# Attention backward on one core: the token stage takes heads four apart, in longer DMA pieces, and ScalarE copies the memory columns

## Chip, cores, metric

The kernel runs on one core of one Trainium2 chip. The metric is the device time of one execution in microseconds, the median of several runs. Engines are named as in the profile: PE (TensorE matmul), PEld (its weight loads), DVE (VectorE), ACT (ScalarE), POOL (GpSimd), SP (SyncE). A "q" behind a name is that engine's instruction queue, which also issues DMAs.

## What is computed

The reference is a gated mix of two attentions over 2048 tokens of width 576, and the gradients of everything but one input. The part that the change touches is the second, a recurrent one with memory:

```python
# H = 32 heads of 128, M = 8 memory rows, segments of 32 tokens (64 segments)
for s in range(n_seg):
    h = concatenate([mem, xs], axis=1)              # 8 memory rows and 32 tokens
    q, k, v = h @ Wq, h @ Wk, h @ Wv                # per head
    p = softmax(where(mask, q @ k.T * scale, -1e9)) # tokens causal, memory seen by all
    o = (p @ v) @ Wo
    mem = o[:, :M]
    outs.append(o[:, M:])
```

The first, A, is plain softmax attention with 32 query heads of 18 and one key and value head. The output is `g * a + (1 - g) * b`, and the kernel returns it with eleven gradients.

## The kernel before

The work is a row of stages, each a hand-ordered program (`manual_schedule`): projections; the memory recurrence forward woven with A's first pass; the **token stage** `b_bulk` (L662); the recurrence backward `b_chain_bwd` (L998) woven with A's second pass `a_pass2` (L1893); then the rest of the gradients. Matrices that do not fit into the chip's memory lie in DRAM tensors between the stages.

The token stage does attention B for the 32 tokens of each segment, forward and backward. Its unit is a *step*: one token tile of 128 tokens (four segments) and four heads. There are 16 tiles x 8 head groups = 128 steps, and `order` (L914) gives, for turn t, which parts of which steps run: a part with lag n works on step t - n, so up to six steps are in flight. A part transposes q, k, dO, v on PE (`trans`, L768), makes scores S against the tokens (diagonal 32x32 blocks) and against the memory columns (`score`, L782), takes exp on ACT (`st_S`), masks and sums on DVE, makes the probabilities P on POOL (`st_R`, L807), the output o and the gradient dq (`attend`, L762), dS on POOL (`st_Y`, L874), and the gradients of the memory rows of k and v (`st_K`, `st_KE`, L893, L901). For every tensor index 0 of P and dS is the tokens' half and index 1 the memory's.

Four steps are a *chunk*: 16 heads of one token tile. Inputs come by chunk, in 512 KB DMAs with 4 KB per token row (`load`, L676): q, dO, k into rings of four, v into three buffers. Memory rows come as `mB` (L693), four DMAs each for k and v, one per place i of a head in its step, into the block of 32 partitions that i owns; memory columns as `mT` (L690), one DMA for each tile and tensor. Results leave by chunk: o, dq (4 KB a row), px and dsx (the tokens' half of P and dS), and the memory gradients dm (four DMAs, L907). Which load follows which part stands in `after` (L917); stores are put on a list (`due`) and issued on SP at the end of the next turn by `flush` (L728), on ACT in the last turns. SP issues in program order.

`mem_T` (L744) transposes on PE the memory's half of P of one step and of dS of another into free columns of the score bank, and copies both to x_mT; `attend_m` (L757) uses x_mT as weights, with mB as the moving side. A step's heads are neighbours: step g of a tile takes heads 4g to 4g + 3, so a chunk's P tile has the order (step, half, place, key).

At the end, `a_pass2` starts with the load of b_KV (L1901) and the first b_QS (L1911), and `b_chain_bwd` reads the memory gradients in `load_c` (L1031).

Of the kernel before, what the change touches and what calls it, by code (L numbers as in the profile page):

```python
# [16 lines left out]
P = 128  # L17
# [29 lines left out]
class Kern:  # L47
# [290 lines left out]
    def b_chain_fwd(self, keep, sp, psum):  # L338
# [69 lines left out]
        for s in range(NSEG):  # L408
# [21 lines left out]
            def mT_store(w):  # L430
                nc.gpsimd.dma_start(self.mTd[w][s], mT[w][:].rearrange("p c u t -> p (c u) t"))
# [230 lines left out]
    def b_bulk(self, wp, vp, kp, sp, psum):  # L662
# [51 lines left out]
        def view(t):  # L714
            return t // 8, t % 8, slice(4 * (t % 4), 4 * (t % 4) + 4), C[t // 4]
# [3 lines left out]
        def store(t, dst, src):  # L719
            if t % 4 == 3:  # L720
                tt, h0 = t // 8, 16 * (t // 4 % 2)
                if len(dst.shape) == 4:
                    due[1].append((dst[tt][:, h0:h0 + 16, :].rearrange("p (a i) k -> p a (i k)", i=4),
                                   src[:, :, 0].rearrange("p a i k -> p a (i k)")))
# [14 lines left out]
        def transp(x, nm):  # L739
            o = sp.tile([P, 4, 32], BF16, name=nm, bufs=2)  # L740
            nc.vector.transpose(o[:].rearrange("p i k -> p (i k)"), x.rearrange("p i k -> p (i k)"))
            return o

        def mem_T(t):  # L744
# [6 lines left out]
            for j, n, w in u:  # L751
                self.tr(pt[:, j, :], C[n // 4][w][:, n % 4, 1].rearrange("p i k -> p (i k)"), P)
                sc[w + "mT", n] = mt[:, j, :]
            js = slice(u[0][0], u[-1][0] + 1)
            nc.vector.tensor_copy(mt[:, js, :], pt[:, js, :])

        def attend_m(t, w, m):  # L757
            po = sc["po" + w, t] = psum.tile([P, 4, P], F32, name="x_po", bufs=2)
            self.mm(po[:].rearrange("p i e -> p (i e)"), lhsT=sc.pop((w + "mT", t)), rhs=m.rearrange("p i e -> p (i e)"),
                    start=True, stop=False)  # L760
# [7 lines left out]
        def trans(t, w, nb):  # L768
            tt, g, r, d = view(t)
# [12 lines left out]
        def score(t, ps, l4, r4, w, part):  # L782
            tt, g, r, d = view(t)
            for i in range(4):
                if part:
                    self.mm(ps[:, 1, i, :], lhsT=l4[:, i, :], rhs=mT[tt][w][:, :, 4 * g + i, :])
# [14 lines left out]

        def st_M(t):
# [4 lines left out]
        def st_R(t):  # L807
            tt, g, r, d = view(t)
# [5 lines left out]
            o = chunk(t, "P", [P, 4, 2, 4, 32], 3)  # L814
            nc.gpsimd.tensor_tensor(out=o[:, t % 4], in0=Et[:], in1=bc(rl[:]), op=ALU.mult)
            store(t, self.px_dram, o)

        def st_T(t):
            sc["PT", t] = transp(view(t)[3]["P"][:, t % 4, 0], "x_PT")

        st_Om = lambda t: attend_m(t, "P", mB["v"][t // 4 % 2][:, t % 4])
        st_Qm = lambda t: attend_m(t, "dS", mB["k"][t // 4 % 2][:, t % 4])

        def st_O(t):
            tt, g, r, d = view(t)
            o = chunk(t, "o", [P, 16, P], 2)
            attend(o[:, r, :], t, "P", sc.pop(("PT", t)), d["v"][:, r, :])
            store(t, self.xtok["o"], o)

        def st_OT(t):  # L830
            tt, g, r, d = view(t)
            pt = psum.tile([P, 4, P], BF16, name="x_tr", bufs=2)
            for i in range(4):
                self.tr(pt[:, i, :], d["o"][:, 4 * (g % 4) + i, :], P)
# [5 lines left out]
        def st_B(t, a):  # L840
            tt, g, r, d = view(t)
# [3 lines left out]
            for i in (2 * a, 2 * a + 1):  # L845
                for hf in range(2):
                    self.mm(pb[tt][:, hf, 0:288], lhsT=oT[:, i, :], rhs=self.WoN[:, 4 * g + i, 288 * hf:288 * hf + 288],
# [16 lines left out]
        def st_D(t):  # L864
            tt, g, r, d = view(t)
# [3 lines left out]
            nc.vector.scalar_tensor_tensor(out=flat(X[:]), in0=flat(ps), scalar=SCALEB, in1=flat(d["P"][:, t % 4]),  # L869
# [4 lines left out]
        def st_Y(t):  # L874
            tt, g, r, d = view(t)
            Y = sp.tile([P, 2, 4, 32], F32, name="x_Y", bufs=1)
            nc.gpsimd.tensor_tensor(out=Y[:], in0=d["P"][:, t % 4], in1=bc(sc.pop(("dl", t))[:]), op=ALU.mult)
            o = chunk(t, "dS", [P, 4, 2, 4, 32], 3)
            nc.gpsimd.tensor_tensor(out=o[:, t % 4], in0=sc.pop(("X", t))[:], in1=Y[:], op=ALU.subtract)
            store(t, self.dsx_dram, o)  # L880

        def st_DT(t):
            sc["DT", t] = transp(view(t)[3]["dS"][:, t % 4, 0], "x_DT")

        def st_Q(t):
            tt, g, r, d = view(t)
            dq = chunk(t, "dq", [P, 16, P], 2)
            attend(dq[:, r, :], t, "dS", sc.pop(("DT", t)), d["k"][:, r, :])
# [4 lines left out]
        def st_K(t):  # L893
            tt, g, r, d = view(t)
            pk = sc["D"][:, 256:512].rearrange("p (x e) -> p x e", e=P)
            for x, (s_, r_) in enumerate((("dS", "q"), ("P", "dO"))):
                for i in range(4):
                    self.mm(pk[32 * i:32 * i + 32, x, :], lhsT=d[s_][:, t % 4, 1, i, :], rhs=d[r_][:, 4 * (g % 4) + i, :],
                            tp=(0, 32 * i))

        def st_KE(t):  # L901
            tt, g, r, d = view(t)
            dm = chunk(t, "dm", [P, 4, 2, P], 2)
            nc.scalar.copy(dm[:, g % 4], sc["D"][:, 256:512].rearrange("p (x e) -> p x e", e=P))
            if t % 4 == 3:
                c2 = t // 4 % 2
# [9 lines left out]
        load(0, ("q", "k", "mT", "dO"))  # L916
        load(1, deep)  # L917
        load(0, ("v", "vB", "kB"))
# [79 lines left out]
    def b_chain_bwd(self, wot, sp, kd, kvp, keep, psum):  # L998
# [16 lines left out]
        def load_a(s, L):  # L1015
            L["vmT"] = sp.tile([P, HB, 8], BF16, name="r_vmT", bufs=1)
            nc.sync.dma_start(L["vmT"][:], self.mTd["v"][s])
# [875 lines left out]
    def a_pass2(self, keep, sp, kvp, psum):  # L1893
# [4 lines left out]
        def load_KV(kb):  # L1898
            if kb < 4:
                KV[kb] = keep.tile([P, 512], BF16, name="b_KV", bufs=2)  # L1900
                nc.sync.dma_start(KV[kb][:], self.kv_dram[:, kb * 512:kb * 512 + 512])  # L1901
# [5 lines left out]
        def load(c):  # L1907
            if c < NC:
                p, q4 = (c // 4) % NPR, c % 4
                QS = sp.tile([P, 2, 512], BF16, name="b_QS", bufs=3)  # L1910
                nc.sync.dma_start(QS[:], self.qs_dram[p, q4])  # L1911
# [322 lines left out]
```

## Time and profile before

| | |
|---|---|
| median of 3 runs | 5436.0 us (5425.35 to 5441.47) |
| the profiled execution | 5450.0 us, its span 5448.3 us |
| PE, PEld busy | 93%, 54% of the span |
| DVE, ACT, POOL busy | 67%, 61%, 44% |
| DMA | 961.44 MB, 176 GB/s; 692,275 of 1,118,175 packets under 512 B |
| HBM | 521.16 MB read, 357.96 MB written |
| token stage | 2138 to 2749 us |
| recurrence backward with A's second pass | 2760 to 4425 us |

A row of the profile gives the line, the engine and the operation, what it writes and reads by the program's names, and a duration. "Idle before" is the time in which the engine had nothing to run, with what ended it; "issue" stands for time in which the engine waited for nothing that the profile shows. In tables of windows there are, after the stretch and its length, busy time and number of instructions of each engine, the clock granted to PE (1.00 is full) and the busy share and rate of the 16 DMA engines. Times within the execution are counted from its first instruction.

### The profile page before, as it was taken

How to read it: one execution, taken by the hardware profiler on the slowest of the kernel's cores; microseconds unless marked ns; L12 is line 12 of the kernel's file. 1: busy time of each engine (PE TensorE's matmuls, PEld its weight loads, DVE VectorE, ACT ScalarE, POOL GpSimd, SP SyncE). 2: the span in 40 equal slices, each digit the busy share in tenths (PEclk: the TensorE clock that was granted, in tenths of full speed). 3: DMA queues.
4: the chain of work that ended last, by engine and by line, in shares of the span. 5: the costliest groups of instructions: out<-in, count | busy, mean ns of one | idle time of the engine just before them, and what ended most of it. 6: DMA issues, size and time to landing. Idle time of an engine off the chain costs nothing.

```text
span 5448.3 us, 218047 instructions
## 1 busy us (share of the span) xinstructions
PE 5055.0 (93%) x93298; PEld 2951.0 (54%) x93476; DVE 3625.4 (67%) x7133; ACT 3329.4 (61%) x4816; POOL 2408.8 (44%) x4632
## 2 busy tenths in 40 slices
PE   7999999999999998888869999999998899999998
PEld 6434555555455555777735555555554467764444
DVE  5337888888888887777768888888888841111112
ACT  4327777887788876666658888788887742111101
POOL 4004555555555554444435666666654321222223
PEclk9999999999999999999989999999999999999999
DMA  6656776766676555878775899888886779976553
GB/s 215 226 181 139 136 134 131 140 136 134 131 140 131 113 109 145 239 230 235 233 227 153 187 202 198 193 194 193 194 181 141 146 158 227 259 235 215 192 178 105
DMA packets 1118175, 961.44 MB, mean 176 GB/s; under 512 B 692275, under 2 KB 944700, under 8 KB 1107603
## 3 DMA queue, kind: packets, MB, share of 16 engines
q1 hardware_dynamic: 1012578, 701.92, 55.4%
q0 software_dynamic: 100016, 242.38, 15.6%
q8 instruction: 731, 11.98, 1.0%
q10 hardware_dynamic: 4608, 3.20, 0.2%
q14 instruction: 242, 1.97, 0.1%
HBM read 521.16 MB, written 357.96 MB: 161 GB/s over the span
## 4 chain that ended last, share of the span: by engine, by line
PE 52%; issue 8%; ACT 6%; POOL 3%; DMA 3%; DVE 0%; SPq 0%; POOLq 0%; ACTq 0%; DVEq 0%
PE w_acc L82 12%; PE r_pj L82 7%; PE b_S L82 6%; PE b_acc L82 5%; PE r_x L82 5%; ACT b_E L1930 4%; PE x_tr L87 3%; PE x_b L82 2%; PE x_po L82 2%; PE a_acc L82 2%; PE a_S L82 2%; PE c_pj L82 1%; PE c_x L82 1%; ACT a_E L1774 1%; DMA b_QS<-qs_dram 1%
## 5 line engine op out<-in xcount | busy, mean ns | idle before, releaser
L1807 DVE TENSOR_TENSOR a_W<-a_dP,a_E 128x512 bf16<-128x512 f32 x2048 | 1315.5, 684 | 264.5 <-issue 121.9
L1953 DVE TENSOR_TENSOR b_dS<-b_dP,b_E 128x512 bf16<-128x512 f32 x2048 | 1311.8, 684 | 236.4 <-issue 96.8
L1930 ACT ACTIVATE b_E<-b_S 128x1024 bf16<-128x1024 f32 x1024 | 1048.2, 1024 | 294.0 <-PE b_dP L82 214.6
L1774 ACT ACTIVATE a_E<-a_S 128x1024 bf16<-128x1024 f32 x1024 | 1049.4, 1025 | 257.9 <-PE a_dP L82 182.8
L82 PEld LDWEIGHTS <-b_QS 32*128 32x128 bf16 (+1 forms) x8192 | 266.4, 92 | 540.6 <-issue 477.8
L82 PE MATMUL r_pj<-WT,r_dT 128*32 128x288 bf16 x12288 | 492.4, 287 | 5.6 <-issue 5.5
L82 PE MATMUL b_S<-b_KV,b_QS 32*128 32x512 bf16 x2048 | 404.2, 383 | 96.5 <-ACT b_E L1930 64.6
L82 PE MATMUL w_acc<-w_d,w_h 128*128 128x512 bf16 (+1 forms) x2352 | 470.9, 379 | 2.5
L82 PE MATMUL a_S<-a_QD,l_KV 32*128 32x512 bf16 x2048 | 402.7, 384 | 54.6 <-ACT a_E L1774 40.6
L82 PE MATMUL b_acc<-b_dS,b_QS 128*32 128x512 bf16 x2048 | 425.0, 393 | 0.2
L82 PE MATMUL a_acc<-a_E,l_VK 128*32 128x256 bf16 x8192 | 404.9, 275 | 7.3 <-issue 2.3
L82 PE MATMUL b_acc<-b_E,b_QS 128*32 128x512 bf16 x2048 | 407.1, 393 | 0.3 <-issue 0.3
L82 PE MATMUL b_dP<-b_KV,b_QS 32*128 32x512 bf16 x2048 | 402.8, 388 | 0.2 <-DVE b_dS L1953 0.2
L82 PE MATMUL a_dP<-a_QD,l_KV 32*128 32x512 bf16 x2048 | 401.8, 388 | 0.8 <-issue 0.7
L82 PEld LDWEIGHTS <-r_dT 128*32 128x32 bf16 x12288 | 331.7, 97 | 101.5 <-issue 9.5
L82 PEld LDWEIGHTS <-w_h 128*128 128x128 bf16 (+1 forms) x2688 | 229.8, 100 | 258.4 <-issue 6.6
L82 PEld LDWEIGHTS <-l_KV 32*128 32x128 bf16 x4096 | 146.5, 91 | 306.4 <-issue 286.0
L82 PE MATMUL a_acc<-a_W,l_WK 128*32 128x256 bf16 x4096 | 304.9, 284 | 1.2 <-issue 0.7
L79 ACT CAST w_o<-w_acc 128x512 bf16<-128x512 f32 x54 | 31.6, 585 | 384.3 <-PE w_acc L82 363.5
L77 DVE CAST w_o<-w_acc 128x512 bf16<-128x512 f32 x54 | 37.4, 692 | 333.4 <-PE w_acc L82 305.0
L1088 POOL TENSOR_TENSOR r_kb<-r_ks,bmask 128x512 bf16<-128x512 bf16 x176 | 188.6, 1072 | 126.9 <-DMA r_ks<-px_dram 45.3
L82 PEld LDWEIGHTS <-hm 128*32 128x32 bf16 x7680 | 202.1, 97 | 78.1 <-issue 9.5
(462 smaller groups left out, 10644.6 us busy)
## 6 DMA issues: line engine op xcount, KB each, us to landing
b_QS<-qs_dram SPq DMA_DIRECT2D x256, 256.0 KB
dOx_dram<-p_tok SPq DMA_DIRECT2D x16, 1024.0 KB
c_vx<-vx_dram SPq DMA_DIRECT2D x64, 256.0 KB
krow_dram<-c_k POOLq DMA_DIRECT2D x64, 256.0 KB
qrow_dram<-c_q POOLq DMA_DIRECT2D x64, 256.0 KB
vrow_dram<-c_v POOLq DMA_DIRECT2D x64, 256.0 KB
x_q<-qx_dram SPq DMA_DIRECT2D x32, 512.0 KB
x_k<-kx_dram SPq DMA_DIRECT2D x32, 512.0 KB
```

Source lines behind the costliest of these rows:

```text
L77: nc.vector.tensor_copy(out, in_)
L79: nc.scalar.copy(out, in_)
L82: return self.nc.tensor.matmul(out, lhsT, rhs, start=start, stop=stop, tile_position=tp, skip_group_check=True)
L87: return self.nc.tensor.transpose(out, in_, self.identB[b:b + nrows, b:b + nrows], tile_position=tp)
L1088: nc.gpsimd.tensor_tensor(out=B[:], in0=a[:].unsqueeze(2).to_broadcast([P, 4, 4, SEG]), in1=self.bmask[:, :, 0].unsqueeze(1).unsqueeze(3). ...
L1774: nc.scalar.activation(E_[n][:], S.pop(n)[:], ACT.Exp, scale=SCALEA)
L1807: nc.vector.tensor_tensor(out=W_[n][:, i, :], in0=dP[i][:], in1=E_[n][:, i, :], op=ALU.mult)
L1930: nc.scalar.activation(E_[n][:], S.pop(n)[:], ACT.Exp, scale=SCALEA)
L1953: nc.vector.tensor_tensor(out=D_[n][:, i, :], in0=dP[i][:], in1=E_[n][:, i, :], op=ALU.mult)
```

## The change

A step now takes heads four apart. Step a of a chunk (a = 0 to 3) has heads 16c + 4i + a for its places i = 0 to 3. So place i owns four neighbouring heads over the chunk, and what is stored or loaded per place is contiguous:

- mB: each of the four DMAs moves 32 rows of 512 neighbouring elements instead of 32 x 4 pieces of 128. The moving side of `attend_m` is then four blocks of 128 with a stride.
- mT: the DRAM tensor has the four segments of a tile within a partition, so a load moves 1024 elements a partition instead of 4 x 256. The stage before stores into it in pieces of the same size as before.
- dm: the DRAM tensor has the tile's own layout; one store of 1024 elements a partition instead of four of 4 x 256. `load_c` reads it with two DMAs (32 x 1024 each) instead of one.
- P and dS: POOL writes each step's P and dS into a small tile (5 and 3 buffers), and then copies the tokens' half into the chunk's tile (place, step, key), from which one store moves 512 elements a partition instead of 4 x 128.
- `mem_T`'s copy is made by ACT instead of DVE.
- At the start v of chunk 0 is loaded ahead of chunk 1's q, dO, k. At the end b_KV and the first two b_QS are issued on ACT's queue instead of SP's.

```diff
-        self.mTd = {w: t(w + "mT_dram", [NSEG, P, HB, 8]) for w in ("k", "v")}
+        self.mTd = {w: t(w + "mT_dram", [NSEG // 4, P, 4, HB, 8]) for w in ("k", "v")}
-        self.dmx_dram = t("dmx_dram", [NM, HB, 2, E])
+        self.dmx_dram = t("dmx_dram", [NTT, 2, P, 4, 2, E])
...
-                            nc.sync.dma_start(mT[tt][x][:], self.mTd[x][4 * tt:4 * tt + 4].rearrange("s p h t -> p s h t"))
+                            nc.sync.dma_start(mT[tt][x][:], self.mTd[x][tt])
...
-                            mB[w[0]][c % 2][32 * i:32 * i + 32, :, i, :],
-                            self.mtok[w[0]][tt * 32:(tt + 1) * 32, h0 * P:h0 * P + 2048]
-                            .rearrange("r (g i e) -> r g i e", i=4, e=E)[:, :, i, :])
+                            mB[w[0]][c % 2][32 * i:32 * i + 32, i].rearrange("p a e -> p (a e)"),
+                            self.mtok[w[0]][tt * 32:(tt + 1) * 32, h0 * P + 512 * i:h0 * P + 512 * i + 512])
...
+        def of_step(tile, t):
+            return tile.rearrange("p (i a) e -> p a i e", a=4)[:, t % 4]
+
+        def head(t, i):
+            return 16 * (t // 4 % 2) + 4 * i + t % 4
...
-            nc.vector.tensor_copy(mt[:, js, :], pt[:, js, :])
+            nc.scalar.copy(mt[:, js, :], pt[:, js, :])
...
-                self.tr(pt[:, i, :], d[w][:, 4 * (g % 4) + i, :], P)
+                self.tr(pt[:, i, :], d[w][:, 4 * i + a, :], P)
...
+        def keep_rows(t, dst, w, o):
+            x = chunk(t, w, [P, 4, 4, 32], 2)
+            nc.gpsimd.tensor_copy(x[:, :, t % 4, :], o[:, 0])
+            store(t, dst, x)
...
-            o = chunk(t, "P", [P, 4, 2, 4, 32], 3)
-            nc.gpsimd.tensor_tensor(out=o[:, t % 4], in0=Et[:], in1=bc(rl[:]), op=ALU.mult)
-            store(t, self.px_dram, o)
+            o = sc["P", t] = sp.tile([P, 2, 4, 32], BF16, name="x_P", bufs=5)
+            nc.gpsimd.tensor_tensor(out=o[:], in0=Et[:], in1=bc(rl[:]), op=ALU.mult)
+            keep_rows(t, self.px_dram, "Px", o)
...
-                for i in range(4):
-                    dst = self.dmx_dram[tt * 32:(tt + 1) * 32].rearrange("m (g i) w e -> i m g (w e)", i=4)
-                    due[1].append((dst[i][:, 4 * c2:4 * c2 + 4, :], dm[32 * i:32 * i + 32].rearrange("p g w e -> p g (w e)")))
+                due[1].append((self.dmx_dram[tt, t // 4 % 2].rearrange("p a w e -> p (a w e)"),
+                               dm[:].rearrange("p a w e -> p (a w e)")))
...
         load(0, ("q", "k", "mT", "dO"))
+        load(0, ("v",))
         load(1, deep)
-        load(0, ("v", "vB", "kB"))
+        load(0, ("vB", "kB"))
...
-            nc.sync.dma_start(mrow["dx"][0:32].rearrange("p u e -> p (u e)"),
-                              self.dmx_dram[s * 8:s * 8 + 8].rearrange("m (c u) w e -> (m c) (u w e)", u=8))
+            src = self.dmx_dram[s // 4].rearrange("b (i u m) a w e -> m b i u (a w e)", u=2, m=32)[8 * (s % 4):8 * (s % 4) + 8]
+            for u in range(2):
+                nc.sync.dma_start(mrow["dx"][0:32, 4 * u:4 * u + 4].rearrange("p a x -> p (a x)"),
+                                  src[:, :, :, u].rearrange("m b i x -> m (b i) x"))
...
-                nc.sync.dma_start(KV[kb][:], self.kv_dram[:, kb * 512:kb * 512 + 512])
+                (nc.sync if kb else nc.scalar).dma_start(KV[kb][:], self.kv_dram[:, kb * 512:kb * 512 + 512])
...
-                nc.sync.dma_start(QS[:], self.qs_dram[p, q4])
+                (nc.sync if c > 1 else nc.scalar).dma_start(QS[:], self.qs_dram[p, q4])
```

`st_Y` is changed for dS as `st_R` is for P, with 3 buffers; `st_O`, `st_Q`, `st_OT`, `st_K`, `st_B` take their heads by `of_step`, `head` or `4 * i + a`.

More of the change, by code (lines that the diff above doesn't have):

```diff
@@ L430, in mT_store @@
             def mT_store(w):
-                nc.gpsimd.dma_start(self.mTd[w][s], mT[w][:].rearrange("p c u t -> p (c u) t"))
+                nc.gpsimd.dma_start(self.mTd[w][s // 4][:, s % 4], mT[w][:].rearrange("p c u t -> p (c u) t"))
             pj = {}
@@ L714, in view @@
         def view(t):
[L715 removed]
+            return t // 8, t % 4, C[t // 4]
+        def of_step(tile, t):
+            return tile.rearrange("p (i a) e -> p a i e", a=4)[:, t % 4]
+        def head(t, i):
+            return 16 * (t // 4 % 2) + 4 * i + t % 4
         due = [[], []]
@@ L721, in store @@
                 tt, h0 = t // 8, 16 * (t // 4 % 2)
-                if len(dst.shape) == 4:
-                    due[1].append((dst[tt][:, h0:h0 + 16, :].rearrange("p (a i) k -> p a (i k)", i=4),
-                                   src[:, :, 0].rearrange("p a i k -> p a (i k)")))
+                if dst.shape[-1] == SEG:
+                    due[1].append((dst[tt][:, h0:h0 + 16, :].rearrange("p h k -> p (h k)"),
+                                   src[:].rearrange("p i a k -> p (i a k)")))
                 else:
@@ L740, in transp @@
             o = sp.tile([P, 4, 32], BF16, name=nm, bufs=2)
-            nc.vector.transpose(o[:].rearrange("p i k -> p (i k)"), x.rearrange("p i k -> p (i k)"))
+            nc.vector.transpose(o[:], x)
             return o
@@ L751, in mem_T @@
             for j, n, w in u:
-                self.tr(pt[:, j, :], C[n // 4][w][:, n % 4, 1].rearrange("p i k -> p (i k)"), P)
+                self.tr(pt[:, j, :], sc[w, n][:, 1].rearrange("p i k -> p (i k)"), P)
                 sc[w + "mT", n] = mt[:, j, :]
             js = slice(u[0][0], u[-1][0] + 1)
-            nc.vector.tensor_copy(mt[:, js, :], pt[:, js, :])
+            nc.scalar.copy(mt[:, js, :], pt[:, js, :])
         def attend_m(t, w, m):
             po = sc["po" + w, t] = psum.tile([P, 4, P], F32, name="x_po", bufs=2)
-            self.mm(po[:].rearrange("p i e -> p (i e)"), lhsT=sc.pop((w + "mT", t)), rhs=m.rearrange("p i e -> p (i e)"),
-                    start=True, stop=False)
+            self.mm(po[:], lhsT=sc.pop((w + "mT", t)), rhs=m, start=True, stop=False)
         def attend(o, t, w, PT, v):
@@ L768, in trans @@
         def trans(t, w, nb):
-            tt, g, r, d = view(t)
+            tt, a, d = view(t)
             pt = psum.tile([P, 4, P], BF16, name="x_tr", bufs=2)
             for i in range(4):
-                self.tr(pt[:, i, :], d[w][:, 4 * (g % 4) + i, :], P)
+                self.tr(pt[:, i, :], d[w][:, 4 * i + a, :], P)
             o = sp.tile([P, 4, P], BF16, name=f"x_{w}T", bufs=nb)
@@ L782, in score @@
         def score(t, ps, l4, r4, w, part):
-            tt, g, r, d = view(t)
             for i in range(4):
                 if part:
-                    self.mm(ps[:, 1, i, :], lhsT=l4[:, i, :], rhs=mT[tt][w][:, :, 4 * g + i, :])
+                    self.mm(ps[:, 1, i, :], lhsT=l4[:, i, :], rhs=mT[t // 8][w][:, :, head(t, i), :])
                     continue
@@ L807, in st_R @@
         def st_R(t):
-            tt, g, r, d = view(t)
             Et = sc.pop(("E", t))
@@ L813, in st_R @@
             nc.vector.reciprocal(rl[:], l[:])
-            o = chunk(t, "P", [P, 4, 2, 4, 32], 3)
-            nc.gpsimd.tensor_tensor(out=o[:, t % 4], in0=Et[:], in1=bc(rl[:]), op=ALU.mult)
-            store(t, self.px_dram, o)
+            o = sc["P", t] = sp.tile([P, 2, 4, 32], BF16, name="x_P", bufs=5)
+            nc.gpsimd.tensor_tensor(out=o[:], in0=Et[:], in1=bc(rl[:]), op=ALU.mult)
+            keep_rows(t, self.px_dram, "Px", o)
         def st_T(t):
-            sc["PT", t] = transp(view(t)[3]["P"][:, t % 4, 0], "x_PT")
-        st_Om = lambda t: attend_m(t, "P", mB["v"][t // 4 % 2][:, t % 4])
-        st_Qm = lambda t: attend_m(t, "dS", mB["k"][t // 4 % 2][:, t % 4])
+            sc["PT", t] = transp(sc["P", t][:, 0], "x_PT")
+        st_Om = lambda t: attend_m(t, "P", mB["v"][t // 4 % 2][:, :, t % 4, :])
+        st_Qm = lambda t: attend_m(t, "dS", mB["k"][t // 4 % 2][:, :, t % 4, :])
         def st_O(t):
-            tt, g, r, d = view(t)
+            d = view(t)[2]
             o = chunk(t, "o", [P, 16, P], 2)
-            attend(o[:, r, :], t, "P", sc.pop(("PT", t)), d["v"][:, r, :])
+            attend(of_step(o[:], t), t, "P", sc.pop(("PT", t)), of_step(d["v"], t))
             store(t, self.xtok["o"], o)
         def st_OT(t):
-            tt, g, r, d = view(t)
+            tt, a, d = view(t)
             pt = psum.tile([P, 4, P], BF16, name="x_tr", bufs=2)
             for i in range(4):
-                self.tr(pt[:, i, :], d["o"][:, 4 * (g % 4) + i, :], P)
+                self.tr(pt[:, i, :], d["o"][:, 4 * i + a, :], P)
             sc["oT", t] = sp.tile([P, 4, P], BF16, name="x_oT", bufs=3)
@@ L840, in st_B @@
         def st_B(t, a):
-            tt, g, r, d = view(t)
+            tt, g = t // 8, t % 8
             oT = sc["oT", t]
@@ L846, in st_B @@
                 for hf in range(2):
-                    self.mm(pb[tt][:, hf, 0:288], lhsT=oT[:, i, :], rhs=self.WoN[:, 4 * g + i, 288 * hf:288 * hf + 288],
+                    self.mm(pb[tt][:, hf, 0:288], lhsT=oT[:, i, :], rhs=self.WoN[:, head(t, i), 288 * hf:288 * hf + 288],
                             start=(g == 0 and i == 0), stop=(g == 7 and i == 3))
@@ L864, in st_D @@
         def st_D(t):
-            tt, g, r, d = view(t)
             ps = half(sc["D"], 0)
@@ L868, in st_D @@
             X = sc["X", t] = sp.tile([P, 2, 4, 32], F32, name="x_X", bufs=2)
-            nc.vector.scalar_tensor_tensor(out=flat(X[:]), in0=flat(ps), scalar=SCALEB, in1=flat(d["P"][:, t % 4]),
+            nc.vector.scalar_tensor_tensor(out=flat(X[:]), in0=flat(ps), scalar=SCALEB, in1=flat(sc["P", t][:]),
                                            op0=ALU.mult, op1=ALU.mult)
@@ L874, in st_Y @@
         def st_Y(t):
-            tt, g, r, d = view(t)
             Y = sp.tile([P, 2, 4, 32], F32, name="x_Y", bufs=1)
[L877 to L880, printed above, removed]
+            nc.gpsimd.tensor_tensor(out=Y[:], in0=sc["P", t][:], in1=bc(sc.pop(("dl", t))[:]), op=ALU.mult)
+            o = sc["dS", t] = sp.tile([P, 2, 4, 32], BF16, name="x_dS", bufs=3)
+            nc.gpsimd.tensor_tensor(out=o[:], in0=sc.pop(("X", t))[:], in1=Y[:], op=ALU.subtract)
+            keep_rows(t, self.dsx_dram, "dSx", o)
         def st_DT(t):
-            sc["DT", t] = transp(view(t)[3]["dS"][:, t % 4, 0], "x_DT")
+            sc["DT", t] = transp(sc["dS", t][:, 0], "x_DT")
         def st_Q(t):
-            tt, g, r, d = view(t)
+            d = view(t)[2]
             dq = chunk(t, "dq", [P, 16, P], 2)
-            attend(dq[:, r, :], t, "dS", sc.pop(("DT", t)), d["k"][:, r, :])
+            attend(of_step(dq[:], t), t, "dS", sc.pop(("DT", t)), of_step(d["k"], t))
             store(t, self.xtok["dq"], dq)
@@ L893, in st_K @@
         def st_K(t):
-            tt, g, r, d = view(t)
+            tt, a, d = view(t)
+            src = {w: sc.pop((w, t)) for w in ("P", "dS")}
             pk = sc["D"][:, 256:512].rearrange("p (x e) -> p x e", e=P)
@@ L897, in st_K @@
                 for i in range(4):
-                    self.mm(pk[32 * i:32 * i + 32, x, :], lhsT=d[s_][:, t % 4, 1, i, :], rhs=d[r_][:, 4 * (g % 4) + i, :],
+                    self.mm(pk[32 * i:32 * i + 32, x, :], lhsT=src[s_][:, 1, i, :], rhs=d[r_][:, 4 * i + a, :],
                             tp=(0, 32 * i))
         def st_KE(t):
-            tt, g, r, d = view(t)
+            tt, a, d = view(t)
             dm = chunk(t, "dm", [P, 4, 2, P], 2)
-            nc.scalar.copy(dm[:, g % 4], sc["D"][:, 256:512].rearrange("p (x e) -> p x e", e=P))
+            nc.scalar.copy(dm[:, a], sc["D"][:, 256:512].rearrange("p (x e) -> p x e", e=P))
             if t % 4 == 3:
-                c2 = t // 4 % 2
-                for i in range(4):
-                    dst = self.dmx_dram[tt * 32:(tt + 1) * 32].rearrange("m (g i) w e -> i m g (w e)", i=4)
-                    due[1].append((dst[i][:, 4 * c2:4 * c2 + 4, :], dm[32 * i:32 * i + 32].rearrange("p g w e -> p g (w e)")))
+                due[1].append((self.dmx_dram[tt, t // 4 % 2].rearrange("p a w e -> p (a w e)"),
+                               dm[:].rearrange("p a w e -> p (a w e)")))
         order = [(2, st_M), (0, st_QT), (None, mem_T), (5, st_B0), (0, st_KT), (4, st_Y), (5, st_B1), (4, st_OT),
@@ L1016, in load_a @@
             L["vmT"] = sp.tile([P, HB, 8], BF16, name="r_vmT", bufs=1)
-            nc.sync.dma_start(L["vmT"][:], self.mTd["v"][s])
+            nc.sync.dma_start(L["vmT"][:], self.mTd["v"][s // 4][:, s % 4])
             L["vxT"] = sp.tile([P, HB, 32], BF16, name="r_vxT", bufs=1)
```

## The prediction

> **What bounds the kernel now.** I read the page first (TensorE, PE, is busy 93% of 5448.3 us; no other engine passes 67%), then the stretch that the change rewrites. The tiles of the token stage (x_D, x_po, x_S) begin at 2138 us and end at 2749 us; 2160 to 2745 us is its steady part. In the table of windows (us, then busy us and instructions of PE, PEld, DVE, ACT, POOL, then granted clock, DMA share, GB/s):
>
> ```profile
> 2160.00:2745.00 585.00, 514.29 (x13872) 425.55 (x13952) 421.49 (x1388) 357.15 (x763) 247.59 (x383) 0.97 0.78 232
> ```
>
> ```profile
> 2644.50:2660.20 15.70, 15.54 (x459) 13.21 (x448) 13.37 (x45) 11.21 (x25) 7.92 (x13) 1.00 0.83 233
> 2660.20:2678.00 17.80, 15.98 (x469) 13.32 (x455) 13.67 (x45) 11.78 (x26) 7.72 (x13) 1.00 0.93 282
> ```
>
> The second fence holds four steps each. The first of them is undisturbed: 15.7 us, 3.93 a step, PE busy all through. The mean step (start of one x_X to the next, 128 of them) is 4.66 us. So PE's own work is a floor of 128 x 3.93 = 503 us, and about 128 x 0.73 = 93 us are lost on top. The waits of that window tell to what:
>
> ```profile
> PE x_D L82 <- issue: 18.9, 15, 2.8
> PE x_po L82 <- issue: 15.6, 16, 2.7
> PE x_b L82 <- issue: 9.3, 5, 2.4
> PE x_tr L87 <- issue: 8.5, 7, 2.7
> PE x_tr L87 <- ACT x_dOT L79: 4.5, 15, 0.3
> ```
>
> Nearly all is "issue": no semaphore. With PE and PEld taken together there are 42 such waits over 0.4 us, 57.9 us in sum (59.9 with the shorter ones). They fall at arbitrary matmuls, but 255, 511, 765, 1020 or 1531 PE instructions apart, that is, every 256th; and each ends 1.2 to 1.7 us after a 16 KB packet of the DMA queue called "instruction" has ended. PE is waiting for its own program. The DMA view of the window:
>
> ```profile
> q1 hardware_dynamic: 127685, 133.23, 76.6%
> q8 instruction: 111, 1.82, 1.3%
> ```
>
> 111 fetches in 585 us; q1 is SP's queue, whose traffic they share the 16 DMA engines with. Counted from PE's entry into the block before, a fetch's packet starts 1.4 us later on average where PE does not stall and 3.7 us where it does; the limit is near 2.1 us. The stalls cost a second time, in granted clock:
>
> ```profile
> 2384.00:2391.50 7.50, 5.49 (x184) 4.54 (x184) 5.35 (x18) 5.14 (x11) 3.30 (x6) 1.00 0.90 275
> 2391.50:2398.50 7.00, 5.84 (x52) 4.38 (x51) 2.36 (x8) 1.18 (x3) 1.22 (x2) 0.52 0.74 179
> ```
>
> After the stall of 2.7 us that ends at 2392.7 the clock is halved for 7 us. Over the stage the granted clock is 0.968 (0.96 to 0.98 in its four quarters), so 585 x 0.032 = 18.7 us. **Instruction fetch behind data transfers costs 59.9 + 18.7 = 79 us of this stage**; the change can win there, and lose there.
>
> **The change, part by part.**
>
> *Longer pieces.* Sizes from the DMA records of 2160 to 2740 us: a 256 B piece takes 18.2 ns of a DMA engine, 512 B 28.7, 2304 B 93.6, a 4096 B row piece 204 (median 159). Memory rows (mB) and P, dS go from 65,536 pieces of 256 B to 16,384 of 1 KB; memory columns (mT) and gradients (dm) from 32,768 of 512 B to 8,192 of 2 KB. Before: 65,536 x 18.2/16 + 32,768 x 28.7/16 = 74.6 + 58.8 = 133 us per engine. No row has 1 KB: between 28.7 and 93.6 ns, on the line between 512 and 2304 B 47; 2 KB is 86 (128 such packets on POOL's queue). After: 16,384 x 47/16 + 8,192 x 86/16 = 48 + 44 = 92 us (73 to 140 by the ends). 41 us of 457 go, the share falls from 0.78 to about 0.71. The row transfers (q, k, v, dO, o, dq), 289 us of the 457, stay.
>
> What that is worth: in the 3 us behind the request of a late fetch the small pieces hold 0.175 of the engines' time, 0.53 us. At 92/133 they hold 0.16 us less, so each late fetch comes 0.16 us earlier: 42 x 0.16 = 6.7 us. If all 0.53 us went out of its way, 21.9. Something more than the first is right, since dm goes from four issues to one: the four hold SP for about 2.7 us of every 18.4 (2.80 at 2649.67), three of them some 2.0, so the rows behind them (dq, and vB, v, k, o) are out earlier and stand less upon the next chunk's q. The stalls lie there: 38 of 56 us at requests from 12 us after a q load to 2 us after the next. I take the middle, 0.35 us: 14.7 us, and of the half clock the same part, 14.7/59.9 x 18.7 = 4.6. **-19 us**, ends -9 and -29.
>
> *PE.* Both programs have 186,191 PE rows, the same 256 per fetch; a strided rhs changes no count. 0.
>
> *Memory columns to ACT (mem_T).* DVE loses 128 x 281 ns = 36 us, but nothing in a dense step waits for DVE there. ACT gets 128 copies of 128x256 out of PSUM, priced by x_dm, 372 ns. The copy stands on ACT behind the dq copy and has to be done for PE's load of x_mT:
>
> ```profile
> 2649.81 0.60 ACT L766 CAST x_dq<-x_po 128x512 bf16<-128x512 f32 x1
> ...
> 2649.93 0.28 DVE L755 COPY x_mT<-x_S 128x256 bf16<-128x256 bf16 x1
> ...
> 2650.94 0.15 PEld L82 LDWEIGHTS <-x_mT 128*128 128x128 bf16 x2
> ...
> 2651.25 0.59 ACT L79 COPY x_dOT<-x_tr 128x512 bf16<-128x512 bf16 x1 [0.83 <-PE x_tr L87]
> ```
>
> dq ends at 2650.41, the load is at 2650.94; over 122 steps that distance is never under 0.475 us. 0.372 fits, by 0.1 us. If the copy took the 585 ns of a 128x512 one it would be 0.11 us late in each step, 14 us. I take 0: what it is nearest to is x_dm. ACT's idle 0.8 us before dOT takes up the rest.
>
> *POOL's two copies (keep_rows).* 128x128: between 243 ns (128x64) and 411 (128x256), some 290. From the end of dS to the next P POOL has 0.56 us at the least, from the end of P to Y 0.53, so either fits; uncovered they would be up to 128 x 0.8 = 105 us. P and dS keep tiles of their own (5 and 3 buffers), and the copies' chunks are rewritten 4 steps after their store, as o and dq are today with no wait for it. 0.
>
> *Start.* v of chunk 0 is issued ahead of q, dO, k of chunk 1 (1.3 us of SP). PE's first waits are 4.5 us for x_qT and 7.1 us for POOL's first x_P, not for v. 0.
>
> *End.* SP issues pass 2's first loads, late:
>
> ```profile
> 2751.02 6.92 ACTq L730 DMA_DIRECT2D dmx_dram<-x_dm  x4
> 2751.94 0.32 SPq L1901 DMA_DIRECT2D b_KV<-kv_dram  x1
> ...
> 2754.72 4.22 SPq L1911 DMA_DIRECT2D b_QS<-qs_dram  x2
> ...
> 2759.95 0.12 PEld L82 LDWEIGHTS <-b_QS 32*128 32x128 bf16 x3 [10.60 <-DMA b_QS<-qs_dram]
> ```
>
> On ACT they come behind its last stores, the dq store of 512 KB among them. One dm store instead of four ends that queue about 5 us earlier, near 2754, so the first QS goes out no sooner than 2754.7 and lands in the same crowd (248 to 291 GB/s). I take -1; ends -5 (half of the 10.4 us gap) and +5 (ACT as late as now, 2759.4, plus the 5.2 us of landing).
>
> *load_c.* 64 more issues on SP in the next stage, 64 x 0.53 = 34 us at 0.526 median. There SP itself waits for PE (164 us at L1017, 69 at L1027, 61 at L1911), so each is taken up: 0; uncovered 34.
>
> **Sum:** -19 - 1 = -20 us on the profiled execution's 5450.0, 5430. Its time lies 14.0 us over the median of the runs, 5436.0; there the forecast is **5416 us**.
>
> **The rivals.**
>
> *Only the rows count* (the stalls stay). For: in the 3 us behind a late request 4 KB pieces hold 0.65 of the engines, behind one in time 0.43; for 256 and 512 B it is 0.18 against 0.23, so small pieces do not go with lateness. Against: late fetches start up to 5.5 us after the request, more than one 512 KB transfer, 8 pieces an engine x 204 ns = 1.6 us. Only the end's -1: 5435. The Trainium skill, DMA: Bandwidth & Descriptors, Queues, rings and completion order, states that a DMA engine goes round its queue rows packet by packet, 9 to 17 descriptors as a rule; by that a fetch waits for the row packet in front of it, which this change leaves as it is, and lags of 5.5 us agree only in part.
>
> *Fetches follow the queue's load.* With a wait in proportion to load/(1 - load), 0.78 to 0.71 is 3.55 to 2.45, 31% of 79 us: -24, and with the lower price of 1 KB (73 us, share 0.68) 40%, -32. Less the end's 1: 5411 to 5403. Near the forecast; beyond -29 I count it apart.
>
> *The bursts close up* (slower). Place: SP's order. Today dO and dq leave 4.1 us apart (medians 3.4 and 7.5 us after q), the four dm issues between them; of 41 requests that fall 2 to 8 us after q only 10 were late, 13.7 us. With one dm issue the two rows can go out back to back, and these requests meet two rows. If they then stall as the 32 in the stretch from 12 to 18 us do (26.1 us, 0.82 each): 41 x 0.82 - 13.7 = +20, half clock +6, end -1: 5461. It decides where dq is issued less than about 1.5 us (a row's 1.6) behind dO.
>
> *The ACT copy is late:* +14 on the forecast, 5430. That the pieces do not get longer is excluded: the program's DMA list has 32x512 and 128x512 where it had 32x4x128 and 128x4x128.
>
> **Chances.** About 0.3%, 16.3 us, is what a measurement of this kernel tells from no change. Forecast (-9 to -30) 0.46, a quarter of it short of 16.3 us; load beyond that 0.14; only rows 0.17; ACT 0.06; bursts 0.17, of which 0.02 within 0.3%. Faster 0.35 + 0.14 = 0.49; same 0.11 + 0.17 + 0.06 + 0.02 = 0.36; slower 0.15. The range leaves out about a tenth on each side: 5396 to 5458.
>
> **What would show it.** Right: DMA share near 0.71 in the stage, fewer than 42 waits "issue", under 45 us of them, clock over 0.97, a dense step still 3.93 us. Rows: share down, stalls not. Bursts: more stalls within 8 us after q. ACT: PE waits "x_po <- ACT x_mT". End: the gap before the first b_S, now 10.4 us. It is wrong if the dense step grows, or if POOL waits for the px or dsx stores.

## The result, and the profile after

The changed kernel takes 5469.5 us (median of 9 runs, 5446.1 to 5479.7), the kernel before 5439.2 in the same rounds: ratio 1.0052, 95% interval 1.0034 to 1.0070. It is slower by about 28 us (18 to 38). The prediction, 5416 us with a range to 5458, was wrong in sign. The profiled execution took 5470.6 us, span 5468.6.

By stages, before and after: up to the token stage 2138.5 and 2134.7 us; token stage (first x_S to last x_po) 611.0 and 621.1; gap to the first b_S 10.4 and 14.3; from there to the last b_acc 1661.1 and 1670.9; the rest 1027.3 and 1027.5. The times of one kernel spread over some 30 us, so single profiles are read here for places, and the ratios for sums.

The windows row of the token stage (columns as before), in the kernel after:

```profile
2156.00:2751.00 595.00, 522.04 (x14005) 426.59 (x13994) 397.21 (x1263) 394.27 (x890) 320.52 (x633) 0.97 0.73 231
```

and its DMA queues:

```profile
q1 hardware_dynamic: 57803, 134.23, 70.8%
q8 instruction: 110, 1.80, 1.2%
```

SP's queue carries the same bytes in less than half the packets (57,803 for 127,685), and its share falls from 76.6% to 70.8%. That part came as said. But PE's waits did not follow:

```profile
PE x_po L82 <- issue: 27.9, 16, 2.8
PE x_D L82 <- issue: 16.1, 13, 2.4
PE x_tr L87 <- issue: 9.7, 8, 2.7
...
PE x_S L87 <- POOL x_dSx L807: 2.8, 1, 2.8
...
PE x_po L82 <- ACT x_mT L760: 0.3, 1, 0.3
```

PE's idle time named "issue", PE and PEld taken together, is 64.7 us in the whole stage (59.9 before), and the granted clock stays at 0.97. PE waits once for POOL's new copy and hardly at all for ACT's. What changed is the order in time on SP. One chunk in the kernel before (start, duration, then what is issued):

```profile
2329.01 0.45 SPq L702 DMA_DIRECT2D x_dO<-dOx_dram  x1
2329.55 2.87 SPq L730 DMA_DIRECT2D dmx_dram<-x_dm  x4
2332.52 0.41 SPq L730 DMA_DIRECT2D dqx_dram<-x_dq  x1
```

and after:

```profile
2327.34 0.38 SPq L701 DMA_DIRECT2D x_dO<-dOx_dram  x1
2327.81 0.41 SPq L735 DMA_DIRECT2D dmx_dram<-x_dm  x1
2328.42 1.77 SPq L735 DMA_DIRECT2D dqx_dram<-x_dq  x1
```

dq now starts 1.1 us behind dO in place of 3.5; by medians 1.6 in place of 4.1 (5.1 against 7.5 us behind q). At the end of the stage, in the kernel after:

```profile
2755.92 0.58 ACT L770 CAST x_dq<-x_po 128x512 bf16<-128x512 f32 x1 [0.79 <-PE x_po L82]
...
2757.88 0.41 ACTq L735 DMA_DIRECT2D dqx_dram<-x_dq  x1
2758.32 0.58 ACTq L1908 DMA_DIRECT2D b_KV<-kv_dram  x1
2759.02 4.78 ACTq L1918 DMA_DIRECT2D b_QS<-qs_dram  x2
...
2770.18 0.13 PEld L82 LDWEIGHTS <-b_QS 32*128 32x128 bf16 x3 [14.49 <-DMA b_QS<-qs_dram]
```

The first b_QS leaves 3.1 us after the stage's last x_po, 2.1 us sooner than before (2754.72 against 2749.5: 5.2), but now behind the 512 KB of the dq store, which left behind it in the kernel before:

```profile
2759.03 0.36 ACTq L730 DMA_DIRECT2D dqx_dram<-x_dq  x1
```

It takes 11.2 us to PE's first weight load in place of 5.2. And in the last quarter of the backward stage (the last 256 b_E, from 4015 us before and 4029 after; a step here is one b_E), one step of 16 has become long. Before:

```profile
4247.00 0.52 SPq L1032 DMA_DIRECT2D r_dx<-dmx_dram  x1
...
4248.89 1.02 ACT L1930 ACTIVATE b_E<-b_S 128x1024 bf16<-128x1024 f32 x1 [0.53 <-PE b_dP L82]
4250.08 1.26 SPq L1039 DMA_TRANSPOSE r_dT<-dqx_dram  x1
4250.44 1.02 ACT L1930 ACTIVATE b_E<-b_S 128x1024 bf16<-128x1024 f32 x1 [0.53 <-PE b_dP L82]
```

and after:

```profile
4264.24 1.42 SPq L1039 DMA_DIRECT2D r_dx<-dmx_dram  x2
...
4266.09 1.02 ACT L1937 ACTIVATE b_E<-b_S 128x1024 bf16<-128x1024 f32 x1 [0.53 <-PE b_dP L82]
4268.40 1.27 SPq L1046 DMA_TRANSPOSE r_dT<-dqx_dram  x1
4268.47 1.02 ACT L1937 ACTIVATE b_E<-b_S 128x1024 bf16<-128x1024 f32 x1 [1.35 <-PE b_acc L82]
```

From one b_E to the next there are 1.55 us before, 2.38 here. Over the last 256 b_E, step 4 of 16 (counted from 0) has a mean of 1.57 before and 1.91 after, where nine of its sixteen cases are late, by 0.3 to 1.0 us; their stretch is 402.4 and 409.2 us.

### The profile page after: what moved, and what is told of

Same layout as the page of the kernel before. It is cut to its first block, busy times and chain, and to the rows that moved or that the text cites. A ratio compares the mean times of both kernels' runs of the same rounds, so it can differ in the third digit from the quotient of the medians.

```text
span 5468.6 us, 218349 instructions
## 1 busy us (share of the span) xinstructions
PE 5069.1 (93%) x93391; PEld 2954.1 (54%) x93476; DVE 3599.3 (66%) x7003; ACT 3368.0 (62%) x4946; POOL 2483.2 (45%) x4888
## 5 line engine op out<-in xcount | busy, mean ns | idle before, releaser
L1937 ACT ACTIVATE b_E<-b_S 128x1024 bf16<-128x1024 f32 x1024 | 1048.2, 1024 | 305.1 <-PE b_dP L82 211.5
```

The costliest lines, as they stand in the source:

```text
L1937: nc.scalar.activation(E_[n][:], S.pop(n)[:], ACT.Exp, scale=SCALEA)
```

## The experiments

Two theories of the token stage. **Rows that stand together**: a fetch of program is late by the row transfers in front of it, so time freed between them is lost again if they move up. **Only the rows count**, wherever they stand. Beside them stand the small shares: the end, load_c, the two copies. "Stalls" are the waits "issue" over 0.4 us from the third x_X to the last but one; "2 to 8" and "12 to 18" are the stalls of fetches requested so many us behind a q load (a fetch counts as requested when PE enters the block of 256 instructions before the one fetched); "last 256" is the stretch of the last 256 b_E; "gap" is that ahead of the first b_S. All in us. A cell of one profile is uncertain by several us: "12 to 18" lies between 21.3 and 31.3 in the thirteen kernels in which k's load has its old place. The ratios are uncertain by some 0.0015 to 0.002, and a difference of two ratios by some 0.002 (11 us).

| kernel | ratio to before (95%) | stalls | 2 to 8 | 12 to 18 | gap | last 256 |
|---|---|---|---|---|---|---|
| before (shown profile) | | 57.9 | 13.7 | 22.1 | 10.4 | 402.4 |
| after | 1.0052 (1.0034-1.0070) | 63.5 | 20.5 | 27.7 | 14.3 | 409.2 |
| end_on_sp | 1.0060 (1.0039-1.0081) | 53.4 | 10.6 | 26.6 | 10.2 | 411.3 |
| mT_on_dve | 1.0049 (1.0033-1.0065) | 61.6 | 17.5 | 28.6 | 11.7 | 408.2 |
| dm_four | 1.0026 (1.0009-1.0043) | 55.8 | 19.1 | 23.3 | 16.5 | 411.6 |
| rows_2k | 1.0051 (1.0033-1.0069) | 64.2 | 17.2 | 28.9 | 13.9 | 412.0 |
| three_undone | 1.0021 (1.0006-1.0035) | 61.5 | 14.3 | 28.4 | 10.6 | 402.9 |
| k_earlier | 0.9998 (0.9984-1.0013) | 52.4 | 28.9 | 12.8 | 10.4 | 402.2 |
| dm_alone | 1.0055 (1.0034-1.0076) | 61.1 | 22.7 | 21.3 | 11.0 | 408.1 |
| mT_alone | 1.0002 (0.9988-1.0017) | 52.9 | 13.2 | 24.0 | 10.1 | 401.6 |
| dm_four_b | 1.0003 (0.9989-1.0017) | 44.5 | 9.0 | 28.3 | 9.4 | 407.1 |
| k_between | 0.9986 (0.9972-1.0000) | 43.5 | 20.1 | 9.9 | 10.1 | 402.8 |
| k_between_dm_four | 0.9969 (0.9956-0.9982) | 41.5 | 10.0 | 18.4 | 9.3 | 402.9 |
| before_k_between | 0.9962 (0.9949-0.9975) | 37.8 | 14.1 | 8.6 | 9.9 | 403.6 |
| two_undone | 1.0037 (1.0023-1.0051) | 73.0 | 20.5 | 31.3 | 10.2 | 412.0 |
| two_undone_dm_four | 1.0020 (1.0005-1.0035) | 47.9 | 8.1 | 26.9 | 9.2 | 415.5 |
| two_undone_k_between | 1.0003 (0.9985-1.0021) | 40.7 | 12.2 | 13.3 | 10.2 | 408.5 |
| before_load_c_two | 1.0011 (0.9995-1.0026) | 52.0 | 12.2 | 23.7 | 9.5 | 406.2 |

**end_on_sp** (from after):

```diff
-                (nc.sync if kb else nc.scalar).dma_start(KV[kb][:], ...)
-                (nc.sync if c > 1 else nc.scalar).dma_start(QS[:], ...)
+                nc.sync.dma_start(KV[kb][:], ...)
+                nc.sync.dma_start(QS[:], ...)
```

> The changed kernel with one part undone: b_KV and the first two b_QS are issued on SP again. In the changed kernel the gap from the last x_po to the first b_S is 14.3 us (10.4 before), since the first b_QS stands behind five stores on ACT's queue and is issued at 2759.0, 3.1 us after the last x_po. If the place of issue costs this, the gap goes back to about 10 us and the time falls by 4 us. If the b_QS would land as late from SP (which has five WT loads in front of it), the gap stays at 14 us and the time too.

The gap is 10.2 us. The time does not show so small a step (1.0060). Over all profiles the gap is 11.7 to 16.5 us, 14.1 by mean, where ACT issues these loads (four kernels), and 9.2 to 11.0, mean 10.0, where SP does (fourteen): the end costs 4 us.

**mT_on_dve** (from after) and **mT_alone** (from before) swap `nc.scalar.copy` and `nc.vector.tensor_copy` in `mem_T`.

> The changed kernel with one part undone: DVE makes the copy of the memory columns again, in place of ACT. The waits of PE for ACT's x_mT are 1.0 us in the whole steady stage. If those waits are all, the time moves by less than 2 us. If ACT's fuller program holds PE up in places that do not bear the name of x_mT (the step of 4.1 to 4.2 us that 14 of 128 steps have, none before), the time falls by 3 to 14 us and the steps are 3.93 again.

> The kernel before with one part of the change: ACT copies the memory columns. If the copy fits into ACT's free time as it was predicted: within 3 us of before, and PE's waits for x_mT below 2 us. If it is late: up to 14 us slower.

1.0049 against 1.0052, and 1.0002: the copy on ACT costs nothing that these runs can tell. (The steps of 4.1 to 4.2 us that the first expectation names are fewer in mT_on_dve, 3 where after has 12, without an effect on the time that shows.)

**dm_four** (from after):

```diff
-                due[1].append((self.dmx_dram[tt, c2] ..., dm[:] ...))
+                for i in range(4):
+                    b = slice(32 * i, 32 * i + 32)
+                    due[1].append((self.dmx_dram[tt, c2][b] ..., dm[b] ...))
```

> The changed kernel, but the memory gradients are stored in four DMAs of 32 partitions again (the same 2 KB pieces), so that dq is issued about 4 us behind dO again in place of 1.6. Theory 'bursts close up': the stalls of PE for its program in requests 2 to 8 us after a q load, 20.5 us in the changed kernel and 13.7 before, go back by some 7 us, with the half clock 9 us, and the time falls by 9 us. Theory 'only the rows count' (stalls depend on row pieces, which are the same): within 3 us of the changed kernel, or slower by what the 96 extra issues cost.

0.0026 less than after, 14 us; dq goes out 7.2 us behind q again. Its single profile shows hardly a fall of the stalls at 2 to 8 us (19.1 for 20.5); the pair of two_undone below does.

**rows_2k** (from after): tiles with a gap in the middle of a row, so that a row DMA has pieces of 2 KB.

```diff
-                        d[w] = self.ring(w)[:, 0:2048].rearrange("p (h e) -> p h e", e=P)
+                        d[w] = self.ring(w)[:].rearrange("p (j x) -> p j x", j=2)[:, :, 0:1024]
```

> The changed kernel, but q, k, v, dO, o and dq move in pieces of 2 KB in place of 4 KB (the tiles in SBUF have a gap in the middle of a row; as many DMAs as before). Two 2 KB pieces take 178 ns of a DMA engine, one 4 KB piece 209 by mean, 168 and 159 by median, so the engines' time stays within some 10 per cent. If a fetch of program waits for a number of packets in front of it ('only the rows count', by number), the start of late fetches comes 1 us or more sooner, most stalls go (64 us to 20 to 35) and the time falls by 30 to 50 us. If the stalls go with the bytes that stand in front of the fetch (load, bursts), the time stays within 8 us of the changed kernel.

1.0051, and the fetches start as late as without the edit (those requested 12 to 18 us behind q, where most stalls are: 3.23 us after the request by mean, 3.19 in after), with 104 ns a piece in place of 209. A fetch does not wait for a fixed number of pieces: halving the pieces in front of it changes nothing. The Trainium skill, DMA: Bandwidth & Descriptors, Queues, rings and completion order, has an engine switch between its rings packet by packet, some 9 to 17 descriptors each. Were the wait one such turn of a fixed number of pieces, it would have been halved here, and it was not; a turn that takes in an engine's whole share of one 512 KB DMA (8 pieces of 4 KB or 16 of 2 KB) is not excluded by this run.

**three_undone** (from after): end_on_sp and mT_on_dve, and the gradient rows in DRAM as 32 x 2 x 4 x 1024, so that load_c is one DMA of 32 rows of 4 KB.

```diff
-        self.dmx_dram = t("dmx_dram", [NTT, 2, P, 4, 2, E])
+        self.dmx_dram = t("dmx_dram", [NTT, 32, 2, 4, 1024])
...
+            nc.sync.dma_start(mrow["dx"][0:32]..., self.dmx_dram[s // 4, 8 * (s % 4):8 * (s % 4) + 8].rearrange("m b (i u) x -> (m b i) (u x)", u=2))
```

> The changed kernel with three parts undone together: b_KV and the first b_QS on SP, the copy of x_mT on DVE, and load_c with one DMA a segment (the gradient rows lie in DRAM so that its 32 rows are 4 KB each; the store stays one DMA of 2 KB pieces). Theory 'second issue of load_c': in the last quarter of the recurrence backward the changed kernel and the four runs so far have one step of 16 that takes 1.86 to 2.07 us in place of 1.57 before, 5 to 8 us in sum; with one DMA it is 1.57 again, and the stretch of the last 256 b_E takes 402 us in place of 408 to 412. Together with the end's 4 us and at most 1 of x_mT the time falls by 11 to 13 us against the changed kernel, a ratio to the kernel before near 1.003. Rival (that step is late for another reason, such as where the program's code lies): 1.86 to 2.07 stays, the ratio stays at 1.004 to 1.006.

Step 4 is 1.59 us again, the stretch 402.9, the time 17 us under after (0.0031). A flaw came in with it: the one dm store now goes to 4 x 32 rows. In the sixteen chunks in which no load of memory columns (also 2 KB pieces) runs beside it, its pieces run at most 5 or 6 at a time and end 6.1 us after the issue by median (7 to 18 at a time and 5.0 us in after). two_undone has no such store. The Trainium skill, DMA: Bandwidth & Descriptors, Why a DMA increments its semaphore by 16 and not by 1, says that the slowest dimension sets how many of the 16 engines a DMA uses; a dimension of 4 would give 4. The trace does not name engines; 5 or 6 pieces at a time are near that.

**dm_alone** (from before): dm's layout, its one store and the two DMAs of load_c as in after, and nothing else.

> The kernel before with one part of the change: the memory gradients go to DRAM in one store of 2 KB pieces and load_c reads them with two DMAs. As heads are still neighbours, the gradient rows reach load_c in another order of heads, so the gradients that follow from them are others. Theory 'second issue of load_c': one step of 16 late in the last quarter of the recurrence backward, 1.9 us or more in place of 1.57, and 5 to 8 us slower than before. Theory 'bursts': dq 2 us sooner, stalls in requests 2 to 8 us behind q from 13.7 to 20 us or more, a further 7 to 9 us slower. If neither: within 3 us of before.

Its heads stay neighbours, so the gradient rows reach load_c in another order of heads and the gradients that follow are others: a kernel for times alone. 1.0055: this part alone makes a loss as large as the whole (18 to 41 us by the interval), with step 4 at 1.95 us and 22.7 us of stalls at 2 to 8 us, 18 late fetches of 41 for 10 of 37.

**k_earlier** (from three_undone) moves k's load to `st_T`, **k_between** (from three_undone), **before_k_between** (from before) and **two_undone_k_between** behind the first load of v's memory rows (`vB0` is the first of the four, `vB1` the other three):

```diff
-        after = {st_O: (("vB", 0), ("v", 0)), ..., st_Q: (("kB", 0), ("k", 3))}
+        after = {st_O: (("vB0", 0), ("k", 0), ("vB1", 0), ("v", 0)), ..., st_Q: (("kB", 0),)}
```

> As three_undone, and the row load of k is issued in the middle of a turn, some 4 us ahead of v, in place of 1.1 us behind it, so that v, k and o no longer go out within 2 us. Theory 'rows that stand together make fetches late' (bursts): the requests 12 to 18 us after a q load, which hold 22 to 29 us of stalls in all six profiles, lose about half of it, and the time falls by 10 to 15 us against three_undone. Rival (any row in front of a fetch does it, wherever it stands): the stalls move to 8 to 12 us and their sum stays at 53 to 64 us, the time within 4 us of three_undone.

> As three_undone, and the row load of k is issued behind the first of the four loads of memory rows of v, which has to wait on SP for its buffer: some 9 us behind q, alone between dq (5 us) and v (12 us). In k_earlier it stood 0.7 us behind dq: stalls in requests 2 to 8 us behind q rose from 14.3 to 28.9 us, those of 12 to 18 us fell from 28.4 to 12.8, and the time by 7 us. Theory 'rows that stand together': the fall at 12 to 18 us stays and the rise goes, the sum of stalls is 40 to 48 us, and the time 15 to 22 us under three_undone, ratio 0.998 to 0.9995. Rival (any row in front of a fetch does it): sum 52 to 62 us, ratio 1.000 to 1.002.

> The kernel before, with only the row load of k moved as in k_between: short pieces, all else as before. By 'rows that stand together' 10 to 15 us faster than before, ratio 0.997 to 0.998. Against k_between_dm_four it shows what the longer pieces are worth where rows stand as far apart: if they are worth the predicted 15 to 19 us, this kernel is that much slower than k_between_dm_four; if only the rows count, the two agree within 5 us.

In k_earlier k went out at 5.6 us behind q, 0.7 behind dq: the stalls moved with it, from 28.4 to 12.8 at 12 to 18 us and from 14.3 to 28.9 at 2 to 8. With k at 9.5, alone (k_between), the sum falls to 43.5. This refutes "wherever they stand".

**dm_four_b**, **k_between_dm_four**: three_undone and k_between with dm in four stores.

> As three_undone, but the memory gradients are stored in four DMAs of 32 partitions again (2 KB pieces), so that dq goes out some 2 us later and four DMAs behind dO, as in the kernel before. All loads and stores that the change makes longer are still longer. Theory 'rows that stand together' (one store of dm lets dq close up to dO, and the fetches pay): 8 to 14 us less than three_undone, ratio to before 0.9995 to 1.001. Rival (it is not the place of dq): as three_undone, 1.002.

> k_between and dm_four_b together: long pieces, dq behind four issues, k alone. By 'rows that stand together' the best of all, 8 to 14 us under k_between, ratio 0.996 to 0.998. If dq so comes near k (7 and 9 us), no better than k_between.

With everything longer and dq 7.1 us behind q, the time is that of before (1.0003). With k moved too, long pieces give 5419.6 us and short ones (before_k_between) 5417.7, in the same rounds.

**two_undone** (end_on_sp and mT_on_dve), **two_undone_dm_four**, and with k moved: the same steps without the flaw.

> The changed kernel with b_KV and the first b_QS on SP and x_mT copied by DVE; the memory gradients as in the changed kernel (one store of all 128 partitions, two DMAs in load_c). By the shares so far (end 4 us): 1.004 to 1.005 against the kernel before.

> two_undone with the store of the memory gradients in four DMAs of 32 partitions, same pieces, same layout, dq some 2 us later. If one store costs by letting dq close up to dO: 9 to 15 us under two_undone, ratio 1.002 to 1.003 (what is left is load_c). If the cost in three_undone was that its store lay on few DMA engines: as two_undone, within 4 us.

> two_undone with the row load of k behind the first load of memory rows of v, as in k_between, here with dm's store on all engines. If rows that stand together make the stalls: 15 us or more under two_undone, stalls of requests 12 to 18 us behind q at 8 to 12 us in place of 22 to 29. If not: within 5 us.

The windows rows of two_undone and of two_undone_k_between:

```profile
2158.00:2759.00 601.00, 520.56 (x14010) 426.60 (x13998) 422.26 (x1389) 358.58 (x765) 320.68 (x634) 0.97 0.72 228
```

```profile
2167.00:2722.00 555.00, 507.66 (x13961) 418.27 (x13950) 421.43 (x1388) 357.44 (x763) 319.79 (x632) 0.99 0.76 246
```

The same instructions and bytes, with k 8.5 instead of 13.0 us behind q: the stage is 46 us shorter in these two executions, 18 us by the ratios (0.0034). The DMA share is higher where the stage is shorter; a low share is no sign of few stalls. dm in four takes 0.0017, 9 us, the stalls at 2 to 8 us from 20.5 to 8.1. In all four pairs of one and of four dm stores (after, three_undone, k_between and two_undone, each against its kernel with four) the ratio falls, by 0.0017 to 0.0026; one pair is near its own uncertainty, the four together are not. Four stores do two things at once: they move dq away from dO, and they spread dm's own 256 KB. No run separates these two.

**before_load_c_two** (from before): load_c's one DMA of 32 x 2048 as two of 32 x 1024.

> The kernel before, with load_c's read of the gradient rows as two DMAs of 32 x 1024 elements in place of one of 32 x 2048; the layout, the rows' order and all else as before. If the second DMA on SP makes the late step of the last 256 b_E: step 4 of 16 takes 1.9 us or more in place of 1.57, the stretch 408 to 410 us in place of 402, the time 5 to 8 us over before. If the order of rows in the changed kernel's load does it: 1.57, 402 us, as before.

```profile
4248.12 0.99 SPq L1034 DMA_DIRECT2D r_dx<-dmx_dram  x2
...
4249.91 1.02 ACT L1932 ACTIVATE b_E<-b_S 128x1024 bf16<-128x1024 f32 x1 [0.53 <-PE b_dP L82]
4251.10 1.26 SPq L1041 DMA_TRANSPOSE r_dT<-dqx_dram  x1
4251.46 1.02 ACT L1932 ACTIVATE b_E<-b_S 128x1024 bf16<-128x1024 f32 x1 [0.53 <-PE b_dP L82]
```

Two issues and a step of 1.55 us; step 4 has a mean of 1.57. (The stretch is 406.2, by single late steps at other places.) So the theory of the second issue falls. What all nine kernels with the late step (1.86 to 2.09) share is the other order of load_c's rows, 8 x 4 in place of 32 in a row. How that order makes the step late is not settled. One rival is left untested: in that order the issue itself takes longer, 1.42 us on SP for the two against 0.99 here and 0.52 for the one DMA of the kernel before. The stretch of the nine is 408.1 to 415.5 us, mean 410.7, against 403.5 in the other nine: 7 us.

## Why the prediction was wrong, point by point

**The failed step is "Longer pieces", -19 us.** The DMA time did fall: 1 KB pieces took 49.8 ns (47 put in), 2 KB 89.2 (86), and in the stage 90 us an engine in place of 124, though rows rose from 204 to 209 ns. But the step took the freed time as time that a late fetch comes sooner (0.35 us each), and read "the rows behind them are out earlier" as a gain. In the changed kernel the late fetches start 3.9 us after their request by mean, against 3.7 before: no sooner. The freed time is worth nothing that these runs can tell: dm_four_b against before, 1.0003 (-6 to +9 us); k_between_dm_four against before_k_between, 0.9969 to 0.9962.

**"The bursts close up", given 0.17, is what happened**, where it was placed: dq behind dO, with fetches requested 2 to 8 us after q. Its size was put at +26 us and is 9 to 14 (two_undone and after against their dm_four). Part of that is the count it was worked out from, 41 requests and 32 with 26.1 us; by the count of the table there are 37 and 30 with 22.1 us, which gives some +18 by the same working. Its limit of 1.5 us was near: dq stands 1.6 us behind dO. That dq, and not dm's own bytes, does it is not shown.

**The end, -1, is +4.** The upper end of +5 was named and not taken. The queue on ACT did shorten and the loads did go out earlier, as said, behind the dq store, as said too. What was missed is the price of that place: "lands in the same crowd" took the landing as it was, 5.2 us, and it became 11.2. That the store in front does it is read from the order of issues; end_on_sp, with a gap of 10.2 us, undoes queue and place together. It fits "rows that stand together" without showing it.

**load_c, 0, is +7.** It was priced as issues on SP, which are indeed hidden (before_load_c_two, 1.57). The changed order of rows in the load was not priced at all, nor that each issue takes 0.67 us in it and not the 0.53 put in.

**Right:** no cost from ACT's copy (mT_alone, 1.0002), from POOL's two copies (PE waited 2.8 us once), from the start (PE's longest waits there are 4.4 and 6.7 us, 4.5 and 7.1 before), or on PE (dense step 3.93 us still). "Only the rows count", 0.17, was right that small pieces do not matter and silent on where rows stand.

**The sum:** 9 to 14, 7 and 4 make 20 to 25 of the 28 us (18 to 38). The rest is within the intervals; no run shows more.

A version that beats both kernels is before_k_between: 5417.7 us against 5433.7, 0.9962 (0.9949 to 0.9975), by the place of one load.

## What to carry to other kernels

Where an engine waits for something small that shares the DMA engines with large transfers, ask how far apart the large ones are issued before asking how many bytes or packets there are. An edit that makes issues cheaper moves everything behind them up; write down the new time of each large transfer. And when a layout changes for a store's sake, look at the order in which the load on the other side now walks it.

## What the hardware showed unexpectedly

Moving one 512 KB load by 3.4 to 4.5 us within a chunk of 18 us was worth 0.0034 to 0.0038 (18 to 21 us, each uncertain by some 11) in each of four pairs (before, three_undone, dm_four_b and two_undone, each against the kernel with k between), as much as the whole change was predicted to bring. More than halving the DMA packets of the stage (127,685 on SP's queue before, 59,142 in dm_four_b) was worth nothing where dq stands as far behind dO as before (1.0003).
